# Retention attention: states that change row halves inside their own step, without copies

## The chip, the cores and the metric

One core of one Trainium2 chip runs the whole program. The metric is device microseconds from launch to end; a kernel's time is the median of its runs. The profile is of one execution, whose own time stands beside its span below.

## The reference

Three stages, in fp32:

```
# q, k, v: (4 batches, 8 heads, 576 tokens, 64 dims)
gamma = 1 - 2**(-5 - head)
D     = gamma**(i - j) where i >= j, else 0
attn  = (q @ k.T / 8 * D) @ v                  # retention: causal scores with a decay
x     = attn as (2304 tokens, 512)
h     = x @ w_in                               # 512 -> 2048
x     = (h * clip(h + 3, 0, 6) / 6) @ w_out    # hard-swish MLP, 2048 -> 512
h     = x @ w_in2                              # 512 -> 1024
out   = layer_norm(h * softmax(h)) * g_ln @ w_out2
```

## The kernel before

The 32 heads of all batches are worked on as 16 pairs. A pair's two heads lie in the two row halves (partitions 0 to 63 and 64 to 127; `HEADS` in the code) of the q and k tiles, which hold them transposed. The 576 tokens are cut into chunks of 128 (the last has 64; `CHUNKS`). Inside a chunk the scores are computed and masked; what earlier chunks contribute comes through a 64x64 state per head and chunk: state 0 is u 0, and state c is the state before it, times a decay, plus u c, where u c is the product of chunk c's decayed v and k. The state before a chunk, times the chunk's q, gives the rest of its output.

For each pair `attention()` issues: `scores` (16 matmuls s; ScalarE copies them to st; GpSimd masks st), `load_pair` for the pair three ahead (four DMAs on SyncE's queue: rk, rq, rv, rn), `chunk_states` (matmuls u; VectorE builds state), `prep` (ScalarE scales the next pair's v), `values` of the pair before (matmuls xp<-st), `last_scores` (matmuls z; VectorE writes st4), and `from_states` of the pair before (matmuls xp<-state). VectorE then multiplies xp into xa (L525), ScalarE and GpSimd split xa into two fp32r words, xb (L260, L261), which the first MLP reads. xp, u and z have one PSUM buffer each, so xp of a pair can begin only when xa of the pair before has been taken out, and u when the state chain before has read it.

The output of chunks 1 and 2 is accumulated from the rows of its own head; for chunks 3 and 4 the weights and q lie in the other row half. For chunk 4 the host swaps the halves of q and k. For chunk 3, and for states 2 and 3, VectorE makes the swap with copies into a tile `turned` (lines 461 and 474): two copies of q's chunk 3, and two copies of the two states, a half each.

From pair 2 on, between the pairs, the first MLP's weights are made ready: they come as 64-bit words (wraw, one load for every other pair), ScalarE and VectorE turn them into fp32 (L139, L144, then L147 and L148 on VectorE), and into two fp32r words (L153 on ScalarE, L158 on VectorE or, every third time, on GpSimd). From pair 4 on, six matmuls h of the first MLP are issued with each pair. TensorE's matmuls and most of ScalarE's instructions in this stage keep program order; VectorE's are placed by a scheduler. Pairs 0 to 2 (`early`) are loaded ahead of everything into tiles of another pool. After the attention come the first MLP in token blocks and the second MLP.

Of the kernel before, what the change touches and what calls it, by code (L numbers as in the profile page):

```python
# [9 lines left out]
F32 = mybir.dt.float32  # L10
# [5 lines left out]
ALU = mybir.AluOpType  # L16
AX = mybir.AxisListType

B, H, S, D = 4, 8, 576, 64
NT, DM, DFF, DFF2 = 2304, 512, 2048, 1024  # L20
NH = B * H
NP = DM // 128
# [1 line left out]
NFF2 = DFF2 // 128  # L24
FA = 6
GAMMA = [1.0 - 2.0 ** (-5 - h) for h in range(H)]
N_DEC = H + H // 2 + H // 2
NPAIR = NH // 2
NV = 5
BLOCKS = [(0, 512), (512, 512), (1024, 512), (1536, 512), (2048, 256)]  # L30
# [44 lines left out]
def retention_hardswish_solu_kernel(ctx, tc, kt, qt, kn, vt, w1, w2i, w2o, gln, decay, place, out):  # L75


    nc = tc.nc
    ve, se, ge, te, sy = nc.vector, nc.scalar, nc.gpsimd, nc.tensor, nc.sync
# [301 lines left out]
    pa = tc.alloc_tile_pool(name="pa", bufs=1)  # L381
    ps_a = tc.alloc_tile_pool(name="ps_a", bufs=1, space=bass.MemoryType.PSUM)

    decay_sb = pa.tile([128, N_DEC], F32, name="decay_sb")
    place_sb = p0.tile([128, NP, 128], F32, tag="r", bufs=2, name="place_sb")
# [1 line left out]
    tab_sb = [pa.tile([128, S], F32, name=f"tab_sb{p}") for p in range(NP)]  # L387
    mask4 = pa.tile([128, NP, 64], F32, name="mask4")
    raws, vs, sts, sts4, states, us, xps = {}, {}, {}, {}, {}, {}, {}
    HEADS = [slice(0, 64), slice(64, 128)]  # L390
    CHUNKS = [slice(128 * c, min(128 * c + 128, S)) for c in range(NV)]

    def at_x(c):

        return slice(128 + CHUNKS[c].start, 128 + CHUNKS[c].stop)
# [3 lines left out]
    def mm_a(*args, **kw):  # L399
        keep(nc.tensor.matmul(*args, **kw))  # L400

    def load_pair(pr):

        if pr >= NPAIR:
            return
        early = pr < EARLY
        if early:
            tag = "wi" if pr < 2 else "g"
            rk, rq, rn = [p0.tile([128, n], F32, tag=tag, bufs=FA, name=f"raw{pr}_{i}")
                          for i, n in enumerate((S, S, 512))]  # L410
        else:
            rk = pa.tile([128, S], F32, tag="rk", bufs=3, name=f"rk{pr}")
            rq = pa.tile([128, S], F32, tag="rq", bufs=4, name=f"rq{pr}")
            rn = pa.tile([128, 512], F32, tag="rn", bufs=3, name=f"rn{pr}")
        nc.sync.dma_start(out=rk, in_=kt[pr])
        nc.sync.dma_start(out=rq, in_=qt[pr])
        if early:
            rv = p0.tile([128, 9, D], F32, tag="g", bufs=FA, name=f"rv{pr}")
        else:
            rv = pa.tile([128, 9, D], F32, tag="rv", bufs=3, name=f"rv{pr}")  # L420
        nc.sync.dma_start(out=rv, in_=vt[pr])
        nc.sync.dma_start(out=rn, in_=kn[pr])
        raws[pr] = rk, rq, rn.rearrange("p (c d) -> p c d", d=128), rv

    def prep(pr):
# [13 lines left out]
    def scores(pr):  # L439
# [4 lines left out]
        for c in range(4):  # L444
            for h in range(2):
                mm_a(sp[h][:, CHUNKS[c]], k[HEADS[h], CHUNKS[c]], q[HEADS[h], CHUNKS[c]], start=(c == 0), stop=(c == 3))
        for h in range(2):
# [6 lines left out]
    def chunk_states(pr):  # L454

        rn, v = raws[pr][2], vs[pr]
        up = ps_a.tile([128, 4, 64], F32, tag="u", bufs=1, name=f"u{pr}")
        state = pa.tile([128, 4, 64], F32, tag="state", bufs=2, name=f"state{pr}")
        turned = pa.tile([128, 256], F32, tag="turned", bufs=2, name=f"turned{pr}")
        for h in range(2):  # L460
            ve.tensor_copy(out=turned[HEADS[1 - h], :128], in_=raws[pr][1][HEADS[h], CHUNKS[3]])
        states[pr] = state, turned
        for c in range(4):
            for h in range(2):
                mm_a(up[HEADS[h], c], rn[:, c, HEADS[h]], v[:, 4 * h + c], start=(c == 0), stop=(c == 3))
        at = H + pr % NP
        ve.tensor_copy(out=state[:, 0], in_=up[:, 0])
        for c in range(1, 4):
            ve.scalar_tensor_tensor(  # L469
                out=state[:, c], in0=state[:, c - 1], scalar=decay_sb[:, at:at + 1], in1=up[:, c],  # L470
                op0=ALU.mult, op1=ALU.add,
            )
        for h in range(2):
            ve.tensor_copy(  # L474
                out=turned[HEADS[1 - h], 128:].rearrange("p (c e) -> p c e", e=64), in_=state[HEADS[h], 2:],
            )

    def places():

# [12 lines left out]
    def last_scores(pr):  # L492
# [3 lines left out]
        for h in range(2):  # L496
            mm_a(zp[HEADS[h]], k[HEADS[h], CHUNKS[4]], q[HEADS[h], CHUNKS[4]], start=True, stop=True)
        ve.tensor_tensor(out=st4, in0=zp, in1=mask4[:, pr % NP], op=ALU.mult)

    def values(pr):  # L500
# [3 lines left out]
        for c in range(4):  # L504
            for h in range(2):
                mm_a(xp[HEADS[h], at_x(c)], v[:, 4 * h + c], st[h][:, CHUNKS[c]], start=(c in (0, 3)), stop=False)

    def from_states(pr):
        xp = xps.pop(pr)
        rq, v, (state, turned), st4 = raws.pop(pr)[1], vs.pop(pr), states.pop(pr), sts4.pop(pr)  # L510
        for h in range(2):
            mm_a(xp[HEADS[h], at_x(4)], v[HEADS[1 - h], 8], st4[HEADS[1 - h]], start=False, stop=False)
        for c, w, q in (
            (1, state[:, 0], rq[:, CHUNKS[1]]), (3, turned[:, 128:192], turned[:, :128]),
            (2, state[:, 1], rq[:, CHUNKS[2]]), (4, turned[:, 192:], rq[:, CHUNKS[4]]),
        ):
            for h in range(2):
                r = HEADS[h if c < 3 else 1 - h]
                mm_a(xp[HEADS[h], at_x(c)], w[r], q[r], start=False, stop=(c in (2, 4)))
        evac_x(pr, xp)  # L520

    def evac_x(pr, xp):
        b, p = divmod(pr, NP)
        xa = pa.tile([128, S], F32, tag="xa", bufs=2, name=f"xa{pr}")
        ve.tensor_tensor(out=xa, in0=xp[:, 128:704], in1=tab_sb[p], op=ALU.mult)  # L525
        for t, tc0, s0, m in segments(b * S, S):
            if (t, p) not in xb:
                xb[t, p] = x_tile(t, p)
            split_x(xb[t, p], slice(tc0, tc0 + m), xa[:, s0:s0 + m])

    def attention():

        for pr in range(NPAIR + 1):
            if pr < NPAIR:
                scores(pr)
                idle_mm(N_IDLE.get(pr, 0))
                if pr == 0:
                    places()
                yield pr
                load_pair(pr + EARLY)  # L540
                chunk_states(pr)
                prep(pr + 1)
                if pr < NP:
                    widen(pr)
            if pr:
                values(pr - 1)
            yield pr
            if pr < NPAIR:
                last_scores(pr)
            if pr:  # L550
                from_states(pr - 1)
            yield pr
            if pr == 1:
                tc.keep_in_program_order(nc.sync.dma_start(out=gln_sb, in_=gln))
# [16 lines left out]
    for pr in range(EARLY):  # L571
        load_pair(pr)
# [3 lines left out]
    for h in range(2):  # L576
        ge.affine_select(
            out=mask4[HEADS[h]], in_=mask4[HEADS[h]], compare_op=ALU.is_ge, fill=0.0,
# [115 lines left out]
    last = len(pairs) - 1  # L694
    x2r, x2w, h2, ebuf, stats, us, lnT, turned, lTs = {}, {}, {}, {}, {}, {}, {}, {}, {}
# [215 lines left out]
    ve, se, ge, te, sy = (Pinned(tc, e) for e in (ve, se, ge, te, sy))  # L911
# [59 lines left out]
    for i in range(last + 1):  # L971
        e = [ends[i, p] for p in range(7)]
# [83 lines left out]
```

## Time and profile before

| | |
|---|---|
| runs | 658.96 us median of 3 (658.83 to 660.0) |
| the profiled execution | 659.14 us; its span 657.4 us |
| granted TensorE clock | 1.00 |
| busy in the span | PE 648.0 us (99%), DVE 356.2 (54%), ACT 370.1 (56%), POOL 328.3 (50%) |
| DMA | 112.93 MB, mean 172 GB/s |
| chain that ended last, by engine | PE 89%, DVE 8%, ACT 1%, issue 1% |

PE is TensorE's matmuls, PEld its weight loads, DVE VectorE, ACT ScalarE, POOL GpSimd, SP SyncE. The shares are means over stages; the attention fills about the first 93 us. A busy PE is not PE at its peak, since ends of matmuls are modelled.

### The profile page before, as it was taken

How to read it: one execution, taken by the hardware profiler on the slowest of the kernel's cores; microseconds unless marked ns; L12 is line 12 of the kernel's file. 1: busy time of each engine (PE TensorE's matmuls, PEld its weight loads, DVE VectorE, ACT ScalarE, POOL GpSimd, SP SyncE). 2: the span in 40 equal slices, each digit the busy share in tenths (PEclk: the TensorE clock that was granted, in tenths of full speed). 3: DMA queues.
4: the chain of work that ended last, by engine and by line, in shares of the span. 5: the costliest groups of instructions: out<-in, count | busy, mean ns of one | idle time of the engine just before them, and what ended most of it. 6: DMA issues, size and time to landing. Idle time of an engine off the chain costs nothing.

```text
span 657.4 us, 10671 instructions
## 1 busy us (share of the span) xinstructions
PE 648.0 (99%) x3922; PEld 536.8 (82%) x3922; DVE 356.2 (54%) x666; ACT 370.1 (56%) x653; POOL 328.3 (50%) x342
## 2 busy tenths in 40 slices
PE   9989999999999999999999999999999999999998
PEld 5767778888889988888888888889988888888887
DVE  4888875407111646135465436212487878887750
ACT  5778666538233756146256337305378677778582
POOL 4767662315031425135135004606469899999453
PEclk9999999999999999999999999999999999999999
DMA  9999615449105252367775654239876343534342
GB/s 322 384 277 328 201 63 183 156 134 360 66 0 161 98 161 96 129 220 230 267 251 185 206 178 160 97 121 345 302 194 158 85 105 100 129 81 96 74 100 69
DMA packets 80025, 112.93 MB, mean 172 GB/s; under 512 B 42594, under 2 KB 47458, under 8 KB 79972
## 3 DMA queue, kind: packets, MB, share of 16 engines
q1 hardware_dynamic: 79824, 112.22, 54.1%
q8 instruction: 31, 0.51, 0.3%
q14 instruction: 22, 0.18, 0.1%
q10 hardware_dynamic: 148, 0.01, 0.0%
HBM read 70.80 MB, written 31.98 MB: 156 GB/s over the span
## 4 chain that ended last, share of the span: by engine, by line
PE 89%; DVE 8%; ACT 1%; issue 1%; POOL 0%; DVEq 0%; POOLq 0%; ACTq 0%
PE h L272 28%; PE x L297 20%; PE o L71 15%; PE h L71 13%; PE acc L297 8%; PE x L71 2%; DVE state L469 2%; DVE turned L474 2%; DVE xa L525 1%; DVE wz L148 1%; PE xp L400 1%; PE warm L400 1%; PE s L400 1%; ACT xb L260 1%; DVE w L158 1%
## 5 line engine op out<-in xcount | busy, mean ns | idle before, releaser
L291 POOL TENSOR_TENSOR g<-gf,g 128x512 fp32r<-128x512 f32 (+1 forms) x78 | 96.7, 1240 | 215.6 <-ACT g L290 208.0
L297 PE MATMUL x<-g,w 128*128 128x512 f32 x576 | 132.0, 389 | 0.0
L272 PE MATMUL h<-xb,w 128*128 128x512 f32 (+1 forms) x600 | 130.2, 360 | 1.8 <-POOL w L158 1.8
L297 PEld LDWEIGHTS x<-g,w 128*128 128x128 f32 x576 | 108.1, 188 | 22.5
L272 PEld LDWEIGHTS h<-xb,w 128*128 128x128 f32 x600 | 98.2, 189 | 19.9 <-POOL w L158 2.6
L285 DVE SCALAR_TENSOR_TENSOR gf<-r,h 128x512 f32<-128x512 f32 (+1 forms) x80 | 50.4, 631 | 118.2 <-ACT r L284 104.6
L71 PE MATMUL o<-w,lt 128*128 128x512 f32 (+1 forms) x456 | 103.0, 378 | 0.0
L71 PEld LDWEIGHTS o<-w,lt 128*128 128x128 f32 x456 | 82.4, 188 | 16.3 <-POOL lt L71 0.3
L284 ACT ACTIVATE r<-h,half 128x512 f32<-128x512 f32 (+1 forms) x80 | 50.6, 635 | 63.0 <-PE h L272 63.0
L272 PE MATMUL h<-xB,w 128*128 128x512 f32 x360 | 82.4, 389 | 0.0
L272 PEld LDWEIGHTS h<-xB,w 128*128 128x128 f32 x360 | 67.6, 188 | 14.0
L290 ACT ACTIVATE g<-gf 128x512 fp32r<-128x512 f32 (+1 forms) x78 | 46.1, 591 | 43.4 <-DVE gf L285 38.2
L71 POOL TENSOR_TENSOR lt<-lT,lt 128x512 fp32r<-128x512 f32 x36 | 61.0, 1710 | 13.5 <-ACT lt L71 13.5
L297 PE MATMUL acc<-g,w 128*128 128x512 f32 (+1 forms) x264 | 62.0, 360 | 0.0
L71 ACT ACTIVATE e<-h,stat 128x1024 f32<-128x1024 f32 x36 | 41.3, 1148 | 35.5 <-DVE stat L71 35.3
L297 PEld LDWEIGHTS acc<-g,w 128*128 128x128 f32 x264 | 46.9, 188 | 8.7
L71 PE MATMUL h<-w2t,xt 128*128 128x512 f32 x216 | 53.5, 390 | 0.0
L147 DVE TENSOR_SCALAR wz<-wz 128x512 int32<-128x512 int32 x44 | 28.2, 641 | 40.9 <-ACT wz L139 40.6
L71 PEld LDWEIGHTS h<-w2t,xt 128*128 128x128 f32 x216 | 40.3, 188 | 8.2
L261 POOL TENSOR_TENSOR xb<-xa,xb 128x512 fp32r<-128x512 f32 (+7 forms) x32 | 30.6, 978 | 21.8 <-ACT xb L260 21.8
L71 PE MATMUL h<-w2b,xt 128*128 128x512 f32 x162 | 39.9, 390 | 0.1
L148 DVE CUSTOM_DVE_ANT_0 wz<-wz,wt 128x1024 uint16<-128x1024 uint16 x44 | 36.7, 836 | 5.0
(123 smaller groups left out, 879.7 us busy)
## 6 DMA issues: line engine op xcount, KB each, us to landing
wraw<-in_w_dram SPq DMA_DIRECT2D x32, 512.0 KB, 5.0
xs<-xb SPq DMA_DIRECT2D x12, 512.0 KB, 6.3
xB<-xs SPq DMA_DIRECT2D x12, 512.0 KB, 6.9
rv<-in_vt_dram SPq DMA_DIRECT2D x16, 288.0 KB, 5.3
x2l<-x2s SPq DMA_DIRECT2D x18, 256.0 KB, 3.9
x2f<-x2o SPq DMA_DIRECT2D x18, 256.0 KB, 3.5
x2r<-x2f SPq DMA_DIRECT2D x9, 512.0 KB, 4.0
out_dram<-osb SPq DMA_DIRECT2D x17, 256.0 KB, 2.0
```

The source lines that it names most:

```text
L71: return lambda *args, **kw: self.keep(op(*args, **kw))
L147: ve.tensor_scalar(out=z, in0=z, scalar1=3, scalar2=None, op0=ALU.logical_shift_left)
L148: ve.tensor_tensor(out=z, in0=z, in1=t, op=ALU.add)
L261: ge.tensor_tensor(out=x[:, 1, c], in0=src, in1=f32(x[:, 0, c]), op=ALU.subtract)
L272: mm = nc.tensor.matmul(hp, w1t[ff, 0][:, a, c], xb[t, p][:, b, :n], start=(p == 0 and i == 0), stop=(p == NP - 1 and i == 2),)
L284: se.activation(out=r, in_=hp, func=ACTF.Relu, scale=1.0 / 6.0, bias=half)
L285: ve.scalar_tensor_tensor(out=gf, in0=r, scalar=1.0, in1=hp, op0=ALU.min, op1=ALU.mult)
L290: se.activation(out=g[ff][:, 0], in_=gf, func=ACTF.Copy)
L291: ge.tensor_tensor(out=g[ff][:, 1], in0=gf, in1=f32(g[ff][:, 0]), op=ALU.subtract)
L297: te.matmul(acc, w1t[ff, 1][:, a, c], g[:, b], start=(first and i == 0), stop=(last and i == 2))
L400: keep(nc.tensor.matmul(*args, **kw))
L469: ve.scalar_tensor_tensor(out=state[:, c], in0=state[:, c - 1], scalar=decay_sb[:, at:at + 1], in1=up[:, c], op0=ALU.mult, op1=ALU.add,)
```

## The change

Three things. The u of chunk 3 of a head is put, by the matmul's output columns, into the other row half of the PSUM tile. The step from state 1 to state 2 is done in two half instructions, each reading one row half (state 1, u 2 and the decay) and writing state 2 into the other; the step to state 3 then runs in full width in the swapped halves, with a decay table that the host has swapped too (four more columns of `decay`). And q's chunk 3 with swapped halves is a further 128 columns of q in DRAM: a pair's q is 704 columns wide instead of 576. For pairs 3 to 15 these come with the same DMA; for pairs 0 to 2 they are a DMA of their own behind the pair's other four. The tile `turned` and its copies are gone.

```diff
-            rq = pa.tile([128, S], F32, tag="rq", bufs=4, name=f"rq{pr}")
+            rq = pa.tile([128, S + 128], F32, tag="rq", bufs=4, name=f"rq{pr}")
...
-        nc.sync.dma_start(out=rq, in_=qt[pr])
+        n = S if early else S + 128
+        nc.sync.dma_start(out=rq[:, :n], in_=qt[pr][:, :n])
...
         nc.sync.dma_start(out=rn, in_=kn[pr])
+        if early:
+            nc.sync.dma_start(out=rq[:, n:], in_=qt[pr][:, n:])
...
-        turned = pa.tile([128, 256], F32, tag="turned", bufs=2, name=f"turned{pr}")
-        for h in range(2):
-            ve.tensor_copy(out=turned[HEADS[1 - h], :128], in_=raws[pr][1][HEADS[h], CHUNKS[3]])
...
-                mm_a(up[HEADS[h], c], rn[:, c, HEADS[h]], v[:, 4 * h + c], start=(c == 0), stop=(c == 3))
+                o = HEADS[1 - h if c == 3 else h]
+                mm_a(up[o, c], rn[:, c, HEADS[h]], v[:, 4 * h + c], start=(c == 0), stop=(c == 3))
...
-        for c in range(1, 4):
-            ve.scalar_tensor_tensor(
-                out=state[:, c], in0=state[:, c - 1], scalar=decay_sb[:, at:at + 1], in1=up[:, c],
-                op0=ALU.mult, op1=ALU.add,
-            )
-        for h in range(2):
-            ve.tensor_copy(
-                out=turned[HEADS[1 - h], 128:].rearrange("p (c e) -> p c e", e=64), in_=state[HEADS[h], 2:],
-            )
+        for c, to, at in (
+            (1, ((ALL, ALL),), H + pr % NP), (2, tuple(zip(HEADS, HEADS[::-1])), H + pr % NP),
+            (3, ((ALL, ALL),), H + 2 * NP + pr % NP),
+        ):
+            for i, o in to:
+                ve.scalar_tensor_tensor(
+                    out=state[o, c], in0=state[i, c - 1], scalar=decay_sb[i, at:at + 1], in1=up[i, c],
+                    op0=ALU.mult, op1=ALU.add,
+                )
...
-            (1, state[:, 0], rq[:, CHUNKS[1]]), (3, turned[:, 128:192], turned[:, :128]),
-            (2, state[:, 1], rq[:, CHUNKS[2]]), (4, turned[:, 192:], rq[:, CHUNKS[4]]),
+            (1, state[:, 0], rq[:, CHUNKS[1]]), (3, state[:, 2], rq[:, S:]),
+            (2, state[:, 1], rq[:, CHUNKS[2]]), (4, state[:, 3], rq[:, CHUNKS[4]]),
...
+    qt = np.concatenate([qt, np.roll(qt[:, :, 384:512], D, axis=1)], axis=2)
```

Apart from these instructions the order on each engine is the same in both kernels. On VectorE, around the state chain of pair 6 (numbers behind names are tile numbers), before:

```order
L461 COPY turned_705<-rq_424 64x128 x2
L158 TENSOR_TENSOR w_1_0_663<-wz,w_1_0_663 128x512
L285 SCALAR_TENSOR_TENSOR gf_0_673<-r_0_672,h_0_578 128x512
L467 COPY state_704<-u_703 128x64
L469 SCALAR_TENSOR_TENSOR state_704<-state_704,decay_sb,u_703 128x64 x3
L498 TENSOR_TENSOR st_744<-z_743,mask_116 128x64
L474 COPY turned_705<-state_704 64x128 x2
L525 TENSOR_TENSOR xa_758<-xp_726,tab_sb_113 128x576
```

and after:

```order
L158 TENSOR_TENSOR w_1_0_642<-wz,w_1_0_642 128x512
L285 SCALAR_TENSOR_TENSOR gf_0_652<-r_0_651,h_0_561 128x512
L466 COPY state_683<-u_682 128x64
L472 SCALAR_TENSOR_TENSOR state_683<-state_683,decay_sb,u_682 128x64
L472 SCALAR_TENSOR_TENSOR state_683<-state_683,decay_sb,u_682 64x64 x2
L472 SCALAR_TENSOR_TENSOR state_683<-state_683,decay_sb,u_682 128x64
L497 TENSOR_TENSOR st_719<-z_718,mask_116 128x64
L524 TENSOR_TENSOR xa_733<-xp_701,tab_sb_113 128x576
```

Four copies a pair are gone, and one step has become two half steps; nothing else has changed places. On SyncE's queue, at the program's start, before:

```order
L415 DMA raw_0_134<-in_kt_dram 128x576
L416 DMA raw_1_135<-in_qt_dram 128x576
L421 DMA rv_139<-in_vt_dram 128x576
L422 DMA raw_2_136<-in_kn_dram 128x512
L415 DMA raw_0_142<-in_kt_dram 128x576
```

and after:

```order
L415 DMA raw_0_134<-in_kt_dram 128x576
L417 DMA raw_1_135<-in_qt_dram 128x576
L422 DMA rv_139<-in_vt_dram 128x576
L423 DMA raw_2_136<-in_kn_dram 128x512
L425 DMA raw_1_135<-in_qt_dram 128x128
L415 DMA raw_0_143<-in_kt_dram 128x576
```

Three such DMAs, one behind each of the first three pairs, stand ahead of all later loads.

## Rows read from the trace of the kernel before

**Rows 1.** Stretches: start:end, length, busy us (count) PE PEld DVE ACT POOL, clock, DMA share, GB/s.
```profile
10.00:20.00 10.00, 10.00 (x202) 8.17 (x203) 8.03 (x28) 7.45 (x17) 6.06 (x13) 1.00 1.05 396
...
50.00:60.00 10.00, 9.99 (x156) 7.86 (x156) 8.59 (x22) 6.87 (x17) 6.33 (x8) 1.00 0.94 337
...
92.00:140.00 48.00, 48.00 (x238) 39.21 (x234) 20.67 (x30) 25.78 (x46) 16.07 (x13) 1.00 0.39 131
```

**Rows 2.** Chain that ended last, 48 to 64 us, by line.
```profile
by line: DVE turned L474 20.4%; DVE wz L148 17.1%; DVE state L469 16.2%; DVE xa L525 14.4%; issue 7.8%; ACT xb L260 6.5%; DVE w L158 5.3%; PE xp L400 3.8%; DVE gf L285 3.7%; ACT w L153 3.3%; DVE turned L461 2.8%; DVE wz L147 2.7%; DVE state
```

**Rows 3.** VectorE in order of time: start, us, engine, line, what [idle before <-releaser].
```profile
55.75 0.76 DVE L525 TENSOR_TENSOR xa<-xp,tab_sb 128x576 f32<-128x576 f32 x1
56.54 0.46 DVE L461 COPY turned<-rq 64x128 f32<-64x128 f32 x2
57.87 0.84 DVE L158 TENSOR_TENSOR w<-wz,w 128x512 fp32r<-128x512 f32 x1 [0.88 <-ACT w L153]
...
59.23 0.21 DVE L467 COPY state<-u 128x64 f32<-128x64 f32 x1
59.48 0.91 DVE L469 SCALAR_TENSOR_TENSOR state<-state,decay_sb,u 128x64 f32<-128x64 f32 x3
...
60.54 1.44 DVE L474 COPY turned<-state 64x128 f32<-64x128 f32 x2
62.01 0.76 DVE L525 TENSOR_TENSOR xa<-xp,tab_sb 128x576 f32<-128x576 f32 x1
...
63.85 1.31 DVE L148 CUSTOM_DVE_ANT_0 wz<-wz,wt 128x1024 uint16<-128x1024 uint16 x1
```

**Rows 4.** TensorE in order of time, same columns.
```profile
30.52 1.66 PE L272 MATMUL h<-xb,w 128*128 128x512 f32 x6
...
35.50 1.75 PE L272 MATMUL h<-xb,w 128*128 128x512 f32 x6
...
53.28 1.66 PE L272 MATMUL h<-xb,w 128*128 128x512 f32 x6
...
60.51 1.64 PE L400 MATMUL s<-rq,rk 64*128 64x128 f32 x16 [0.48 <-ACT st L448]
...
64.64 1.66 PE L272 MATMUL h<-xb,w 128*128 128x512 f32 x6
...
87.27 4.41 PE L272 MATMUL h<-xb,w 128*128 128x512 f32 x18
```

**Rows 5.** ScalarE in order of time, same columns.
```profile
59.34 0.63 ACT L290 ACTIVATE g<-gf 128x512 fp32r<-128x512 f32 x1 [0.93 <-DVE gf L285]
59.88 1.06 ACT L448 ACTIVATE st<-s 128x512 f32<-128x512 f32 x2
...
62.44 0.67 ACT L144 ACTIVATE wt<-wraw 128x512 int32<-128x512 uint32 x1
```

**Rows 6.** Instructions on the tile turned: duration ns min/median/max, first and last start.
```profile
L474 DVE COPY turned<-state x32: 220/341/949, 10.8 to 89.5; 64x128 f32<-64x128 f32 x32
L461 DVE COPY turned<-rq x26: 219/222/328, 18.7 to 85.7; 64x128 f32<-64x128 f32 x26
```

**Rows 7.** Instructions on the tile state, same columns.
```profile
L469 DVE SCALAR_TENSOR_TENSOR state<-state,decay_sb,u x48: 272/281/285, 9.9 to 88.4; 128x64 f32<-128x64 f32 x48
```

**Rows 8.** GpSimd in order of time, columns as rows 3.
```profile
60.05 1.27 POOL L291 TENSOR_TENSOR g<-gf,g 128x512 fp32r<-128x512 f32 x1 [0.88 <-ACT g L290]
...
63.61 2.02 POOL L261 TENSOR_TENSOR xb<-xa,xb 128x384 fp32r<-128x384 f32 x2 [1.12 <-ACT xb L260]
```

**Rows 9.** All engines in order of time, 18 to 21 us, columns as rows 3.
```profile
18.31 0.70 ACT L139 ACTIVATE wz<-wraw 128x512 f32<-128x512 f32 x1 [0.28 <-DMA wraw<-in_w_dram]
...
19.91 0.69 DVE L148 CUSTOM_DVE_ANT_0 wz<-wz,wt 128x1024 uint16<-128x1024 uint16 x1
...
20.20 1.81 POOL L261 TENSOR_TENSOR xb<-xa,xb 128x512 fp32r<-128x512 f32 x2 [1.22 <-ACT xb L260]
```

**Rows 10.** Who waited for whom, 12 to 86 us: in total, times, longest.
```profile
ACT wz L139 <- DMA wraw<-in_w_dram: 0.3, 1, 0.3
```

More of the change, by code (lines that the diff above doesn't have):

```diff
@@ L26 @@
 GAMMA = [1.0 - 2.0 ** (-5 - h) for h in range(H)]
-N_DEC = H + H // 2 + H // 2
+N_DEC = H + H // 2 + H // 2 + H // 2
 NPAIR = NH // 2
@@ L389, in retention_hardswish_solu_kernel @@
     raws, vs, sts, sts4, states, us, xps = {}, {}, {}, {}, {}, {}, {}
-    HEADS = [slice(0, 64), slice(64, 128)]
+    HEADS, ALL = [slice(0, 64), slice(64, 128)], slice(0, 128)
     CHUNKS = [slice(128 * c, min(128 * c + 128, S)) for c in range(NV)]
@@ L409, in load_pair @@
             rk, rq, rn = [p0.tile([128, n], F32, tag=tag, bufs=FA, name=f"raw{pr}_{i}")
-                          for i, n in enumerate((S, S, 512))]
+                          for i, n in enumerate((S, S + 128, 512))]
         else:
             rk = pa.tile([128, S], F32, tag="rk", bufs=3, name=f"rk{pr}")
-            rq = pa.tile([128, S], F32, tag="rq", bufs=4, name=f"rq{pr}")
+            rq = pa.tile([128, S + 128], F32, tag="rq", bufs=4, name=f"rq{pr}")
             rn = pa.tile([128, 512], F32, tag="rn", bufs=3, name=f"rn{pr}")
         nc.sync.dma_start(out=rk, in_=kt[pr])
-        nc.sync.dma_start(out=rq, in_=qt[pr])
+        n = S if early else S + 128
+        nc.sync.dma_start(out=rq[:, :n], in_=qt[pr][:, :n])
         if early:
@@ L457, in chunk_states @@
         up = ps_a.tile([128, 4, 64], F32, tag="u", bufs=1, name=f"u{pr}")
-        state = pa.tile([128, 4, 64], F32, tag="state", bufs=2, name=f"state{pr}")
-        turned = pa.tile([128, 256], F32, tag="turned", bufs=2, name=f"turned{pr}")
-        for h in range(2):
-            ve.tensor_copy(out=turned[HEADS[1 - h], :128], in_=raws[pr][1][HEADS[h], CHUNKS[3]])
-        states[pr] = state, turned
+        state = states[pr] = pa.tile([128, 4, 64], F32, tag="state", bufs=2, name=f"state{pr}")
         for c in range(4):
             for h in range(2):
-                mm_a(up[HEADS[h], c], rn[:, c, HEADS[h]], v[:, 4 * h + c], start=(c == 0), stop=(c == 3))
-        at = H + pr % NP
+                o = HEADS[1 - h if c == 3 else h]
+                mm_a(up[o, c], rn[:, c, HEADS[h]], v[:, 4 * h + c], start=(c == 0), stop=(c == 3))
         ve.tensor_copy(out=state[:, 0], in_=up[:, 0])
-        for c in range(1, 4):
-            ve.scalar_tensor_tensor(
-                out=state[:, c], in0=state[:, c - 1], scalar=decay_sb[:, at:at + 1], in1=up[:, c],
-                op0=ALU.mult, op1=ALU.add,
-            )
-        for h in range(2):
-            ve.tensor_copy(
-                out=turned[HEADS[1 - h], 128:].rearrange("p (c e) -> p c e", e=64), in_=state[HEADS[h], 2:],
-            )
+        for c, to, at in (
[7 more added lines that the diff above has]
+                )
     def places():
@@ L509, in from_states @@
         xp = xps.pop(pr)
-        rq, v, (state, turned), st4 = raws.pop(pr)[1], vs.pop(pr), states.pop(pr), sts4.pop(pr)
+        rq, v, state, st4 = raws.pop(pr)[1], vs.pop(pr), states.pop(pr), sts4.pop(pr)
         for h in range(2):
@@ L1041 @@
     last = np.concatenate([last[:64, :, 1], last[64:, :, 0]], axis=0)
-    place, decay = place.astype(np.float32), np.concatenate([over, step, last], axis=1).astype(np.float32)
+    place, decay = place.astype(np.float32), np.concatenate([over, step, last, np.roll(step, D, axis=0)], axis=1).astype(np.float32)
     host = dict(kt=kt, qt=qt, kn=kn, vt=vt, w1=w1, w2i=w2i, w2o=w2o, gln=gln, decay=decay, place=place)
```

## The prediction

> **What bounds the kernel now.** I read the stretches first, to see where TensorE has anything to give. Behind the attention, from 92 to 140 us, PE is busy for 48.00 of 48.00 us [rows 1], and the view of waits names none of PE's behind that: no saving on another engine helps there, but whatever the attention gives up moves the whole rest forward. In the attention PE looks busy too, 9.99 of 10 us from 50 to 60 [rows 1], but a busy PE need not be at its pace; the pace shows in when the same work comes round. Six matmuls h stand once in each pair. From 30.52 to 35.50 a pair takes 4.98 us; the two pairs from 53.28 to 64.64 take 11.36 us together, not 9.96 [rows 4]. From 30.52 to 87.27 there are eleven such groups, so ten pairs in 56.75 us; at 4.98 each they would take 49.8. So 6.95 us can be had there at most, and nothing after.
>
> Next I read the chain, to see what the lost time waits for. From 48 to 64 us it runs mostly on VectorE: turned L474 20.4%, wz L148 17.1%, state 16.2%, xa 14.4% [rows 2]. So, although VectorE is busy for only 8.59 of 10 us [rows 1], its order is the loop that sets the pace. The place where TensorE feels it is in every second pair: s waits 0.48 us for ScalarE's st, and its 16 matmuls then take 1.64 us [rows 4], since the second half of st comes later still. Followed back: st (59.88) stands behind g, which waited 0.93 us for VectorE's gf [rows 5]; gf stands behind w L158, which waited for ScalarE's w, which comes after xa of the pair before [rows 3]. So xa's end sets the time of the next st, and the copies ahead of xa set xa.
>
> **The change, part by part.**
>
> *The copies go.* The two of q's chunk 3 take 0.46 us a pair, the two of the states 1.44 us in the slow pair [rows 3]; the state copies have a median of 341 ns each, a least of 220 and a most of 949 [rows 6]. The long one starts at 60.54, while GpSimd works from 60.05 to 61.32 [rows 8], and the pair of copies ends at 61.98. The steps of the state, which read PSUM besides, took 272 to 285 ns in all 48 cases [rows 7], whatever GpSimd did. So the copies' price is partly a wait for GpSimd, which the half steps should not have.
>
> [...]
>
> *The half steps come.* One step of about 0.31 us with its gap (three take 0.91) becomes two, with half the rows but the same 64 elements along each. I take 0.31 for each; a half step below the least row, 0.22 of a copy across the halves [rows 6], or above 0.86, which a copy needs against GpSimd, would surprise me. So the chain grows from 1.16 us (59.23 to 60.39) to 1.47 [rows 3].
>
> [...]
>
> *Per pair on VectorE:* less 0.46 and 0.57 to 1.44, plus 0.31: 0.7 to 1.6 us off.
>
> *What is late next.* For two pairs, let xa's end (55.75 + 0.76 = 56.51) be zero. ScalarE's chain behind it (xb, w, r, g, st, v, wz, wt) does not get shorter: w and gf hang on xa, not on the copies, and wt ends at 62.44 + 0.67 = 63.11 [rows 3, 5], 6.60 us later. Then L148 can start; before, it started at 63.85, since the copies held VectorE. Behind it come the state chain, 1.47, and with their gaps the mask of z and xa, about 1.0. With L148 at 0.69 the loop is 6.60 + 0.05 + 0.69 + 1.47 + 1.0 = 9.8 us; with L148 at 1.31 it is 10.4. L148 took 0.69 at 19.91, where GpSimd began its xb after it, at 20.20 [rows 9], and 1.31 at 63.85, where GpSimd had begun at 63.61 [rows 3, 8]. After the change L148 is about 0.7 us earlier, and xb on GpSimd is not, since it follows wt on ScalarE; so the row at 19.91 is nearer. TensorE itself needs 9.96 for two pairs. The slower of the two loops decides: 9.96, or 10.4 where GpSimd still wins. I take 10.1. Five times (11.36 - 10.1) is 6.3 us; the ends are 5 x 0.96 = 4.8 and the whole 6.95.
>
> *The u of chunk 3 in the other columns* is as many matmuls as before. The head that comes first now takes the columns that the matmul just ahead of it used. The trace shows no such neighbours. If it must wait for a whole matmul, I estimate the price from s, 16 rows in 1.64 us [rows 4], 0.10 each and twice as wide as u: at most 0.05 a pair, 0.8 us over 16 pairs; at least nothing. I take 0.2.
>
> *The q from DRAM.* 64 KB more for each pair, 1 MB in all. At the start the queue is full: share 1.05, 396 GB/s [rows 1]. Ahead of the first wraw stand three extra DMAs and one longer one, 256 KB or 0.66 us at that rate; as the early ones move rows of only 512 bytes I allow 0.8. ScalarE already waits 0.28 us for that wraw at 18.31 [rows 9], so its wz, and st and s behind it, come up to 0.8 later. TensorE loses that at pair 4; but soon after it needs the first w from VectorE, which hangs on the xa before it, now free of its copies. So most of the 0.8 is hidden there; I charge 0.3, with 0 and 0.8 as ends. Later loads have cover: this was the one wait for a load from 12 to 86 us [rows 10], and a pair is loaded three pairs ahead, some 15 us. SyncE issues three DMAs more, ahead of the other loads, with the queue full anyway. The four more decay columns are 2 KB: nothing.
>
> *Sum:* 6.3 - 0.2 - 0.3 = 5.8 us. The profiled execution took 659.14, its span 657.4; it becomes 653.3. The median, 658.96, is 0.2 lower, so I predict 653.2, a span near 651.6.
>
> **The rivals.**
>
> *GpSimd keeps the lock (22%).* L148 still meets xb in most turns, so the loop is 10.4, and neither the wraw nor the columns are hidden: 4.8 - 0.8 - 0.8 = 3.2 us, 655.9. For it: at 63.85 L148 took 1.31, and a shift of a tenth decides which of two engines is first. Against: wt, not the copies, should now release L148, and xb follows wt.
>
> *All is hidden (10%).* TensorE runs at 4.98 from the start, and pairs 3 to 5, ahead of 30.52, give up 1 us more (at the 0.7 a pair of the later ones they would give 2): 8 us, 651.2. Against: the late wraw.
>
> *The loads become the bound (6%), the other side.* The DMA share is 0.94 at 337 GB/s from 50 to 60 us [rows 1]. If the queue is really full through the attention, each pair's 64 KB costs 0.19 us at that rate, 16 pairs 3.1 us, and the pairs can be no closer than the loads let them: 659.1 + 3.1 = 662.2. It decides from the point where a pair's q lands after its first s. Against: only 0.3 us of waits for loads in all [rows 10].
>
> *Off the path (7%).* The attention ends earlier, but the weights of the second half (wraw, ScalarE, VectorE) do not follow, and TensorE waits for them instead: 659. Against: from 92 to 140 us VectorE is busy for 20.67 of 48 us and DMA at 0.39 [rows 1], and they shift with the attention.
>
> **How the numbers follow.** My own case has 55%, from 651.9 to 654.9 (a gain of 4 to 7). The 80% range reaches into both neighbours: 651.0 to 657.0. About 0.2%, 1.3 us, is what a measurement here can tell from no change. Faster: 0.55 + 0.22 + 0.10, 0.87; the same, mostly the fourth rival, 0.07; slower 0.06.
>
> **What would show it.** In the new profile: no gaps of 0.48 before s in every second pair, and groups of h about 10.1 us apart over two pairs; L148 at about 0.7, started right behind wt; half steps near 0.28; the first wz at about 19.0 instead of 18.31; a PE still without gaps from 87 us on. The prediction is wrong if h stays at 11 us for two pairs (then ScalarE's chain, not VectorE's, was the loop), if s waits for rq or rk, or if gaps open on PE behind 92 us.

## The result, and the profile after

The changed kernel takes 651.04 us (median of 4 runs, 650.53 to 651.58); the kernel before took 658.89 us on the same chip (median of 4 runs; the table above has the first 3). The ratio is 0.9877 [0.9860, 0.9894]: a gain of 7.8 us, where 5.8 were forecast, and the median lies at the lower edge of the range (651.0), 0.9 us below the own case of the forecast (651.9 to 654.9). In a later comparison on another chip the ratio was 0.9875 [0.9862, 0.9887]. The profiled execution took 651.58 us, its span 649.8.

Stretches of the changed kernel, in the columns of [rows 1]:

```profile
50.00:60.00 10.00, 10.00 (x169) 7.86 (x157) 7.08 (x20) 8.68 (x20) 7.41 (x11) 1.00 0.99 337
...
92.00:140.00 48.00, 47.99 (x210) 39.02 (x209) 17.82 (x27) 26.05 (x45) 11.90 (x9) 1.00 0.49 165
```

PE's busy time says as little as before; VectorE is busy for 7.08 us instead of 8.59, and the rest behind the attention is still full. The groups of h show what happened (TensorE in order of time, against [rows 4]):

```profile
30.66 1.66 PE L272 MATMUL h<-xb,w 128*128 128x512 f32 x6
35.54 1.66 PE L272 MATMUL h<-xb,w 128*128 128x512 f32 x6
...
79.40 4.47 PE L272 MATMUL h<-xb,w 128*128 128x512 f32 x18
```

From there every pair takes 4.87 us, none more. The ten pairs from 30.66 to 79.40 take 48.74 us; before they took 56.75. That is 8.0 us; 0.14 was lost ahead of the first of them, and 0.3 behind the last, so the span is 7.6 shorter.

The chain that ended last, 48 to 64 us, by line, in place of [rows 2]:

```profile
by line: PE h L272 29.8%; PE xp L400 29.6%; PE s L400 21.2%; PE u L400 15.4%; PE z L400 4.7%
```

VectorE is gone from it: TensorE waits for nobody. VectorE's own order over one turn of two pairs, against [rows 3]:

```profile
50.38 0.76 DVE L524 TENSOR_TENSOR xa<-xp,tab_sb 128x576 f32<-128x576 f32 x1
52.50 0.83 DVE L158 TENSOR_TENSOR w<-wz,w 128x512 fp32r<-128x512 f32 x1 [1.36 <-ACT w L153]
...
57.20 0.43 DVE L147 TENSOR_SCALAR wz<-wz 128x512 int32<-128x512 int32 x1 [1.09 <-ACT wz L139]
57.77 0.69 DVE L148 CUSTOM_DVE_ANT_0 wz<-wz,wt 128x1024 uint16<-128x1024 uint16 x1 [0.15 <-ACT wt L144]
58.45 0.23 DVE L466 COPY state<-u 128x64 f32<-128x64 f32 x1
58.71 1.21 DVE L472 SCALAR_TENSOR_TENSOR state<-state,decay_sb,u 128x64 f32<-128x64 f32 x4
...
60.12 0.76 DVE L524 TENSOR_TENSOR xa<-xp,tab_sb 128x576 f32<-128x576 f32 x1
```

L148 took 0.69 here, before 1.31, and it waits for ScalarE's wt, as does L147 for wz: in this turn the idle 1.09 us are VectorE's reserve. All seven of L148 from 12 to 86 us (groups of instructions by line: count, busy us, mean ns, idle before):

```profile
L148 DVE CUSTOM_DVE_ANT_0 wz<-wz,wt 128x1024 uint16<-128x1024 uint16 x7 | 4.8, 693 | 1.0 <-ACT wt L144 0.3
```

What ScalarE and then GpSimd do there (in order of time, in the columns of [rows 5] and [rows 8]):

```profile
57.06 0.68 ACT L144 ACTIVATE wt<-wraw 128x512 int32<-128x512 uint32 x1
```

```profile
58.24 1.66 POOL L261 TENSOR_TENSOR xb<-xa,xb 128x384 fp32r<-128x384 f32 x2 [1.10 <-ACT xb L260]
```

L148 began at 57.77, ahead of GpSimd's xb at 58.24; before, 0.24 behind it. The steps of the state, against [rows 7]:

```profile
L472 DVE SCALAR_TENSOR_TENSOR state<-state,decay_sb,u x64: 272/281/289, 9.8 to 79.1; 128x64 f32<-128x64 f32 x32, 64x64 f32<-64x64 f32 x32
```

The half steps (64x64) cost what the full ones cost: four follow one another in 1.21 us, 0.30 each. And the one place where the change lost (all engines in order of time, 18 to 22 us, against [rows 9]):

```profile
19.27 0.68 ACT L139 ACTIVATE wz<-wraw 128x512 f32<-128x512 f32 x1 [0.76 <-DMA wraw<-in_w_dram]
...
21.73 0.48 PE L400 MATMUL s<-rq,rk 64*128 64x128 f32 x2 [1.15 <-ACT st L451]
```

The first wraw is there at 19.27 instead of 18.31, and the st and s behind it on their engines are late with it.

### The profile page after: what moved, and what is told of

Its sections match the earlier page's. It is cut to its first block, busy times and chain, and to the rows that moved or that the text cites. A ratio compares the mean times of both kernels' runs of the same rounds, so it can differ in the third digit from the quotient of the medians.

```text
span 649.8 us, 10629 instructions
## 1 busy us (share of the span) xinstructions
PE 643.9 (99%) x3922; PEld 535.0 (82%) x3922; DVE 334.3 (51%) x618; ACT 370.9 (57%) x653; POOL 325.2 (50%) x342
## 4 chain that ended last, share of the span: by engine, by line
PE 96%; DMA 3%; ACT 0%; SPq 0%; issue 0%; ACTq 0%
PE h L272 31%; PE x L297 20%; PE o L71 15%; PE h L71 13%; PE acc L297 8%; PE xp L400 3%; PE x L71 2%; PE s L400 2%; DMA wraw<-in_w_dram 1%; PE u L400 1%; DMA raw<-in_qt_dram 1%; DMA raw<-in_kn_dram 1%; PE z L400 0%; ACT wt L144 0%; ACT xb L260 0%
## 5 line engine op out<-in xcount | busy, mean ns | idle before, releaser
L147 DVE TENSOR_SCALAR wz<-wz 128x512 int32<-128x512 int32 x44 | 28.8, 653 | 47.0 <-ACT wz L139 46.7
L139 ACT ACTIVATE wz<-wraw 128x512 f32<-128x512 f32 x44 | 29.1, 662 | 18.1 <-DMA wraw<-in_w_dram 9.2
L261 POOL TENSOR_TENSOR xb<-xa,xb 128x512 fp32r<-128x512 f32 (+7 forms) x32 | 28.2, 902 | 16.3 <-ACT xb L260 16.3
```

Source lines behind the costliest of these rows:

```text
L139: first = se.activation(out=z.bitcast(F32), in_=raw[:, :, 1].bitcast(F32), func=ACTF.Prelu, scale=2.0 ** -112, alpha=2.0 ** 32)
L147: ve.tensor_scalar(out=z, in0=z, scalar1=3, scalar2=None, op0=ALU.logical_shift_left)
L261: ge.tensor_tensor(out=x[:, 1, c], in0=src, in1=f32(x[:, 0, c]), op=ALU.subtract)
```

## The experiments

Theory: the gain is VectorE's time on the loop xa, ScalarE, L148, states, xa, part of it time in which the copies wait for GpSimd; the floor under it is TensorE's own pace. Against it stand: the wait for GpSimd is all of it; it is VectorE's time alone, wherever it stands; TensorE gained from what it reads (it no longer reads `turned`); the loads are the floor. Letters in the expectations are those of each text. Times of before are of the same chip as the run beside them.

**One part alone, q.** The q of chunk 3 comes from DRAM; the copies of the states stay (the diff is against the kernel before):

```diff
-            ve.tensor_copy(out=turned[HEADS[1 - h], :128], in_=raws[pr][1][HEADS[h], CHUNKS[3]])
...
-            (1, state[:, 0], rq[:, CHUNKS[1]]), (3, turned[:, 128:192], turned[:, :128]),
+            (1, state[:, 0], rq[:, CHUNKS[1]]), (3, turned[:, :64], rq[:, S:]),
```

> Only the q part of the change: q's chunk 3 from DRAM, the two copies of the states stay. Theory (VectorE's own time ahead of xa sets the pace of two pairs): L148 no longer comes after the q copies, so two pairs take about 10.3 us instead of 11.36, and the time is 653.5 (653 to 654.5). Rival A (the wait for GpSimd in the state copies is nearly all of the gain): these copies still wait, two pairs stay above 11 us, 657 to 659. Rival B (TensorE gains because it no longer reads the tile turned): about half of the gain, 655.

653.89 us against 659.07, ratio 0.9924 [0.9909, 0.9939]. As the theory had it. VectorE around the turn of L148 (in order of time):

```profile
59.85 0.69 DVE L148 CUSTOM_DVE_ANT_0 wz<-wz,wt 128x1024 uint16<-128x1024 uint16 x1
...
60.72 0.92 DVE L470 SCALAR_TENSOR_TENSOR state<-state,decay_sb,u 128x64 f32<-128x64 f32 x3
...
61.78 0.86 DVE L475 COPY turned<-state 64x128 f32<-64x128 f32 x2
62.67 0.76 DVE L526 TENSOR_TENSOR xa<-xp,tab_sb 128x576 f32<-128x576 f32 x1
```

Without the copies of q, L148 has its 0.69 already: from 12 to 86 us it is never longer in this kernel.

**The other part alone, states and columns.** The half steps and the u columns; the two copies of q stay (the diff is against the changed kernel):

```diff
+            ve.tensor_copy(out=turned[HEADS[1 - h]], in_=raws[pr][1][HEADS[h], CHUNKS[3]])
...
-            (1, state[:, 0], rq[:, CHUNKS[1]]), (3, state[:, 2], rq[:, S:]),
+            (1, state[:, 0], rq[:, CHUNKS[1]]), (3, state[:, 2], turned),
```

> Only the state part: half steps and the u of chunk 3 in the other columns; q's two copies on VectorE stay, and no byte more is loaded. Theory: the loop is the changed kernel's 9.75 plus the 0.46 us of the q copies, about 10.2 for two pairs, 653; nothing is lost to loads at the start, so the first h stands no later than the 25.34 of before. Rival A: the wait for GpSimd is gone with the state copies, so nearly the whole gain, 651.3. Rival B: about half, 655.

657.52 us, 0.9973 [0.9962, 0.9983]: above all the numbers given; the h of pair 4 stands at 25.48, not by 25.34. VectorE in order of time shows why:

```profile
51.33 0.69 DVE L148 CUSTOM_DVE_ANT_0 wz<-wz,wt 128x1024 uint16<-128x1024 uint16 x1
...
52.19 1.20 DVE L474 SCALAR_TENSOR_TENSOR state<-state,decay_sb,u 128x64 f32<-128x64 f32 x4
...
53.54 1.15 DVE L461 COPY turned<-rq 64x128 f32<-64x128 f32 x2
54.72 0.76 DVE L526 TENSOR_TENSOR xa<-xp,tab_sb 128x576 f32<-128x576 f32 x1
```

The scheduler put q's copies directly ahead of xa. There the two take 1.15 us, where before, behind xa, they took 0.46 [rows 3]. So this run is no clean removal of one part: it removed the state copies and moved q's to their place. The gains of the parts, 5.2 and 1.6 us, don't add up to 7.8 for that reason.

**Copies put back that nobody reads**, two a pair ahead of xa, once from SBUF and once from PSUM:

```diff
+        for h in range(2):
+            ve.tensor_copy(out=turned[HEADS[1 - h], :].rearrange("p (c e) -> p c e", e=64), in_=state[HEADS[h], 2:])
```

> The changed kernel, plus two copies a pair of states 2 and 3 from the state tile into a tile that nobody reads, at the place where the state copies stood. Theory: VectorE has 1.8 us of idle time to spare in two pairs, but the copies stand ahead of xa: two pairs take 10.2 to 10.6, 653 to 655. Rival A: the copies wait for GpSimd again, up to 0.95 us each, and the time is 656 or more. Rival B: nobody reads the copies on TensorE, so 651.0 as the changed kernel.

```diff
+        for h in range(2):
+            ve.tensor_copy(out=turned[HEADS[1 - h], :].rearrange("p (c e) -> p c e", e=64), in_=up[HEADS[h], 2:])
```

> As the one before, but the two copies read u 2 and u 3 in PSUM, not the state tile in SBUF. Theory: a copy from PSUM should not wait for GpSimd and takes about 0.25 us in every case; what it adds is VectorE's own time, 0.5 a pair, so the time is at or slightly below the kernel with SBUF copies, 652 to 654. Rival A: without the wait for GpSimd no loss at all, 651.0. Rival B: 651.0 too.

From SBUF 657.79 us, 0.9984 [0.9975, 0.9994], above the theory's range: here rival A's number came, 656 or more. From PSUM 654.16, 0.9924 [0.9909, 0.9939], 0.2 above the theory's range and far from the 651.0 of both rivals. The copies (duration ns min/median/max), of the first kernel and of the second:

```profile
L478 DVE COPY turned<-state x32: 220/570/679, 10.0 to 86.9; 64x128 f32<-64x128 f32 x32
```

```profile
L478 DVE COPY turned<-u x32: 283/288/294, 11.3 to 83.3; 64x128 f32<-64x128 f32 x32
```

VectorE and GpSimd of the SBUF version, then of the PSUM version, in the same turn (st's mask stands ahead of the copies in the first, behind them in the second):

```profile
60.05 1.15 DVE L478 COPY turned<-state 64x128 f32<-64x128 f32 x2
```

```profile
59.27 1.27 POOL L291 TENSOR_TENSOR g<-gf,g 128x512 fp32r<-128x512 f32 x1 [0.89 <-ACT g L290]
60.50 1.22 POOL L452 TENSOR_SCALAR_AFFINE_SELECT st<-st 128x512 f32<-128x512 f32 x2
```

```profile
58.13 0.59 DVE L478 COPY turned<-u 64x128 f32<-64x128 f32 x2
```

```profile
57.49 1.29 POOL L291 TENSOR_TENSOR g<-gf,g 128x512 fp32r<-128x512 f32 x1 [0.89 <-ACT g L290]
58.73 1.22 POOL L452 TENSOR_SCALAR_AFFINE_SELECT st<-st 128x512 f32<-128x512 f32 x2
```

In both GpSimd works on through the copies. From SBUF they take 1.15 us, from PSUM 0.59, although a copy from SBUF alone is the shorter one (220 ns against 283). So it is through most of the attention: from 30 to 80 us the 18 copies from SBUF took 574 ns in the mean, the 20 from PSUM 289. Where no GpSimd instruction ran beside them, two copies from SBUF took 0.46 us in the kernel before (56.54 to 57.00 [rows 3]; GpSimd in order of time):

```profile
54.19 1.22 POOL L449 TENSOR_SCALAR_AFFINE_SELECT st<-st 128x512 f32<-128x512 f32 x2
57.15 2.03 POOL L261 TENSOR_TENSOR xb<-xa,xb 128x384 fp32r<-128x384 f32 x2 [1.74 <-ACT xb L260]
```

The two kernels differ by 3.6 us in all: nearly all of it is the price of waiting for GpSimd, more than the theory gave it. The other 3.1 us, from 651.04 to 654.16, are VectorE's time itself, so the wait is not all. Nothing reads these copies: what they cost does not come from TensorE's reading. Why a copy from SBUF takes longer beside GpSimd, no run shows; the wait for GpSimd is a name for that longer time. The pair of runs shows where it comes: same work, same turn, and copies from SBUF take 220 to 679 ns each, while those from PSUM are never stretched (283 to 294 ns).

**All four copies back, unread.**

```diff
+            ve.tensor_copy(out=turned[HEADS[1 - h]], in_=raws[pr][1][HEADS[h], CHUNKS[3]])
...
+            ve.tensor_copy(out=turned[HEADS[1 - h], :].rearrange("p (c e) -> p c e", e=64), in_=state[HEADS[h], 2:])
```

> The changed kernel, with all four copies a pair put back as work that nothing reads: two of q's chunk 3 and two of states 2 and 3, SBUF to SBUF on VectorE, at the places of before. Theory (the gain is VectorE's time and its wait for GpSimd, and nothing else of the change matters): the whole gain goes, two pairs take about 11.3 us again, 658.2 to 660. Rival (what TensorE reads, the u columns, or the loads gave part of it): some of the gain stays, 656.5 or less.

667.77 us against 658.82, 1.0138 [1.0121, 1.0155]: slower than before by 9 us, with the same four copies. Neither number came. The copies did not come back to their places (VectorE in order of time):

```profile
61.93 0.46 DVE L463 COPY turned<-rq 64x128 f32<-64x128 f32 x2
62.42 0.76 DVE L529 TENSOR_TENSOR xa<-xp,tab_sb 128x576 f32<-128x576 f32 x1
64.54 0.82 DVE L158 TENSOR_TENSOR w<-wz,w 128x512 fp32r<-128x512 f32 x1 [1.36 <-ACT w L153]
```

The q copies now stand ahead of xa. Before, they stood behind it, in front of a w that VectorE had to wait 0.88 us for anyway [rows 3], so that one pair in two had them for nothing; now the idle time of 1.36 behind xa stays empty. Two pairs take 12.2 us (a table further below adds up to it). So it is not VectorE's time wherever it stands: nearly the same work in another order is worth 9 us. Half of these are at the start, where h of pair 4 comes at 29.90 us instead of 25.34 (TensorE waited 1.65 and then 1.92 us for xa there; behind the second wait xp took 1.35 us and that h 2.36, one pair later 1.05 and 1.66; the mean granted clock of that execution was 0.997); VectorE waited for loads of q ahead of an xa that needed none (in order of time):

```profile
20.21 0.80 DVE L463 COPY turned<-rq 64x128 f32<-64x128 f32 x2 [1.17 <-DMA rq<-in_qt_dram]
21.04 0.76 DVE L529 TENSOR_TENSOR xa<-xp,tab_sb 128x576 f32<-128x576 f32 x1
```

**More bytes.** Pairs 3 to 15 load 48 KB more each, which nothing reads:

```diff
-            rq = pa.tile([128, S + 128], F32, tag="rq", bufs=4, name=f"rq{pr}")
+            rq = pa.tile([128, S + 224], F32, tag="rq", bufs=4, name=f"rq{pr}")
...
-        n = S if early else S + 128
+        n = S if early else S + 224
```

> The changed kernel itself, unaltered, on the same chip as the next three, as their yardstick. 651.0 us, within 0.5.

> The changed kernel, but the q of pairs 3 to 15 is loaded 96 columns wider still, 48 KB a pair that nothing reads: 0.62 MB more. Theory (4.87 us a pair is TensorE's own pace, and the loads have room below it): h stays 4.87 apart, 651.0, at most 0.3 more at the start. Rival (the loads already set the pace): at the 337 to 359 GB/s of the attention 48 KB take 0.14 us, 13 pairs 1.8 us: 652.8, with waits of s for rq.

The changed kernel again: 650.95 us. With 48 KB more: 650.83, both 0.9875 of before (659.17). Stretch 30 to 70 us, of the changed kernel's first profile and of the wider one:

```profile
30.00:70.00 40.00, 40.00 (x652) 31.86 (x651) 27.65 (x76) 34.45 (x79) 31.16 (x40) 1.00 1.02 364
```

```profile
30.00:70.00 40.00, 40.00 (x631) 31.92 (x630) 27.64 (x74) 34.73 (x80) 31.19 (x41) 1.00 1.02 380
```

A DMA share of 1.02 looks full, and yet 4% more bytes went through and cost nothing: the loads are not the floor. In the four kernels with copies, too, of one or the other kind, the quicker pair of two takes 4.87 us; only in the two kernels with all four copies it takes more.

**The start.** Five kernels that try to win back what the late first wraw costs, by two remedies and both together.

> The changed kernel, but pairs 0 to 2 get their swapped q by two VectorE copies each, as before the change, instead of the three 64 KB DMAs; so 192 KB less stand ahead of the first wraw. Theory (the bytes at the start cost what the attention's start lost): wraw lands about 0.5 us earlier, near 18.7 instead of 19.2; TensorE's wait for st, 1.15 us near 20.6, shrinks by 0.3 to 0.6; every h from pair 4 on comes that much earlier and the pace of 4.87 stays: 650.4 to 650.8. Rival A (that wait comes from elsewhere, the v that waits for rv): time as the changed kernel's, 651.0. Rival B (six copies on VectorE cost more than the bytes): 651.3 or more.

> As the run before, and the first conversion of wraw on ScalarE (wz, wt) is issued behind the next pair's st copy, no longer ahead of it, so that st and TensorE's scores do not stand behind the wait for wraw. Theory (the wait of 1.15 us near 20.6 us is a queue on ScalarE, not a need of data): the wait goes, and every later h comes 0.8 to 1.2 us earlier than in the changed kernel: 649.8 to 650.3. Rival (the first w is then late, and the first h waits for it instead): a new PE wait for w near 24 us, and 651 or more.

> The changed kernel, but the first conversion of wraw (wz, wt on ScalarE) is issued behind the st of pair 3, no longer ahead of it. Theory (TensorE's wait for st near 20.5 us, 0.64 to 1.15 in three profiles of this design, is a queue on ScalarE behind a late load): the wait goes, and with the pace unchanged all that follows comes 0.5 to 1.0 us earlier: 650.0 to 650.4. Rival (the first w, which the first h needs, is then late): a PE wait for w near 25 us of about the same size, 650.8 or more.

> The changed kernel, but pairs 0 to 2 get the swapped q by two ScalarE copies each, issued behind their st copies, where q has long landed, instead of the three 64 KB DMAs. It is the version with VectorE copies with its own fault taken out: there the third copy stood at the head of VectorE's queue waiting for its load, and TensorE waited 3.48 us. Theory (192 KB less ahead of the first wraw): wraw lands 0.5 us earlier, the wait for st at 20.5 us shrinks by about that: 650.4 to 650.7. Rival (six ScalarE copies of about 0.3 us each delay v and st by more than that): 651 to 652.

> Both of the last two: ScalarE copies for pairs 0 to 2 and the first wz behind the st of pair 3. Theory: no wait of TensorE between 5 and 480 us beyond 0.2 us, 649.8 to 650.4; if the first is right and the second wrong, as the late wz alone.

The edits: the first inserts VectorE copies and drops the early DMA, the fourth the same on ScalarE; the third moves the first `wq.begin()`; the second and fifth combine.

```diff
-        if early:
-            nc.sync.dma_start(out=rq[:, n:], in_=qt[pr][:, n:])
...
+                ve.tensor_copy(out=q[HEADS[1 - h], S:], in_=q[HEADS[h], CHUNKS[3]])
```

```diff
-        if pr >= W_FROM and pr % 2 == 0 and s % 3 == 1:
+        if (pr > W_FROM and pr % 2 == 0 and s % 3 == 1) or (pr == W_FROM + 1 and s % 3 == 0):
```

```diff
+                keep(se.activation(out=q[HEADS[1 - h], S:], in_=q[HEADS[h], CHUNKS[3]], func=ACTF.Copy))
```

With VectorE copies 654.48 us (0.9928 [0.9915, 0.9941]), and with the late wz besides 655.14 (0.9943 [0.9931, 0.9955]): 3.5 and 4.2 us slower than the changed kernel: the numbers of the rivals that lie above, but the cause is neither's. VectorE and then TensorE of the first of these:

```profile
11.24 0.81 DVE L462 COPY raw<-raw 64x128 f32<-64x128 f32 x2 [1.98 <-DMA raw<-in_qt_dram]
11.97 0.21 DVE L468 COPY state<-u 128x64 f32<-128x64 f32 x1
```

```profile
13.81 0.79 PE L400 MATMUL u<-v,raw 128*64 128x64 f32 x16 [3.48 <-DVE state L474]
14.32 1.98 PE L400 MATMUL xp<-st,v 128*64 128x128 f32 x16
```

The scheduler let the copy for pair 2 stand at the head of VectorE's queue, where it waits for a load that lands at 11.2, ahead of a state chain whose u was long there; TensorE stood still for 3.48 us. Behind that its granted clock was lower (third column from the end, 15 to 20 us):

```profile
15.00:20.00 5.00, 5.00 (x85) 4.20 (x81) 2.55 (x9) 2.64 (x7) 0.78 (x1) 0.73 1.04 397
```

The xp at 14.32 took 1.98 us; in the changed kernel, with a granted clock of 1.00 from 10 to 20 us, it took 1.04.

With the late wz alone 650.51 us (0.9875 [0.9861, 0.9890]), with ScalarE copies 650.42 (0.9872 [0.9858, 0.9887]), with both 650.78 (0.9877 [0.9863, 0.9892]). The second lies in its theory's range, the first just above it, the third misses it: TensorE waited there 0.28 us for v and 0.60 for xa instead. Two medians lie 0.4 to 0.5 below the changed kernel's 650.95, but no ratio can be told from its 0.9875. In the late-wz kernel s no longer waits for st, 1.15 us in the first profile of the changed kernel (TensorE in order of time):

```profile
20.44 1.16 PE L400 MATMUL s<-rq,rk 64*128 64x128 f32 x16 [0.44 <-DMA rq<-in_qt_dram]
```

It waits for its load instead, 0.44 us. So the queue on ScalarE held st, and the loads stand right behind it. Whether the start can give 0.5 us stays open: in three profiles of the changed start (its two and the wider one's) the h of pair 4 came at 25.62, 25.18 and 24.97 us, which is as much as what was looked for.

## Why the prediction was right in kind and short in size

*The loop was right, and after the change it no longer binds.* From xa's end (51.14) to wt's end (57.74) are 6.60 us, as forecast; with L148 0.69, the state chain 1.47 (58.45 to 59.92) and mask and xa, the next xa ends at 60.88: 9.74 us for two pairs, where 9.8 was worked out for an L148 of 0.69. That these 9.74 are also TensorE's 9.75 is no accident: VectorE waits for TensorE in this turn. The xa at 60.12 stands 0.15 us behind the end of the last xp (TensorE in order of time):

```profile
59.37 0.60 PE L400 MATMUL xp<-rq,state 64*64 64x128 f32 x16
```

So do, by 0.15 to 0.16, all four xa behind an L148 from 50 to 80 us. How long the loop is by itself can be estimated from the kernel with PSUM copies, where xa comes 1.3 us or more after xp and L148 starts right behind wt: 10.18 less its 0.59 of copies is 9.59. To this estimate the other kernels add what they put into the turn of L148 (the one of two pairs in which it stands), and the time by which L148 starts later behind wt than in the changed kernel, since copies in the other turn, or q's copies ahead of L147, use up more than the wait for wz (1.09 us here):

| kernel | us more in the L148 turn | L148 later | 9.59 + both | measured, two pairs |
|---|---|---|---|---|
| changed | 0 | 0 | 9.59 | 9.75 (TensorE's pace) |
| states' copies, 3 steps | 0.86 - 0.30 | 0.14 | 10.29 | 10.31 |
| PSUM copies | 0.59 | 0 | 10.18 (taken from it) | 10.18 |
| SBUF copies | 1.15 | 0.12 | 10.86 | 10.91 |
| q's copies ahead of xa | 1.15 | 0.12 | 10.86 | 10.92 |
| all four copies back | 1.65 | 0.95 | 12.19 | 12.21 |
| before | 0.65 - 0.30, L148 0.69 longer | 0.73 | 11.36 | 11.38 |

(Means of four turns of L148 from 38 to 84 us; measured: eight pairs of h from 30.3 to 35.5 us on, a quarter of them.) All but the changed kernel agree to 0.06, and kernels in which TensorE reads `turned` follow the same sum as those in which nobody does. The last row is the change itself: of what it took from VectorE's loop, 0.73 us is the later start of L148, 0.69 its stretch beside GpSimd, and 0.35 the state copies less the half step.

*The failed step is "I take 10.1"* for the two pairs, a value between 9.96 and 10.4. The L148 of 1.31, from which the 10.4 came, did not occur in the attention: of all kernels run, L148 was stretched ahead of 86 us only in the two with all four copies, and wt releases it now, as the text itself argued. Measured were 9.75, so this choice is 0.35 too long, five times 1.75 us: 0.21 from the floor of 9.96, and 0.14 put on top for an L148 of 1.31.

*Under it lay a wrong floor.* The 4.98 us of the quicker pair [rows 4] was taken as TensorE's own pace. It is 4.87: also the quicker pair of before held 0.11 us of stall, not listed as a wait. TensorE in order of time, before and then after, at the start and in a quick pair:

```profile
14.90 0.69 PE L400 MATMUL u<-v,raw 128*64 128x64 f32 x16
15.42 1.04 PE L400 MATMUL xp<-st,v 128*64 128x128 f32 x16
...
33.20 0.69 PE L400 MATMUL u<-v,rn 128*64 128x64 f32 x16
33.77 1.09 PE L400 MATMUL xp<-st,v 128*64 128x128 f32 x16
```

```profile
14.59 0.69 PE L400 MATMUL u<-v,raw 128*64 128x64 f32 x16
15.11 1.04 PE L400 MATMUL xp<-st,v 128*64 128x128 f32 x16
...
57.71 0.69 PE L400 MATMUL u<-v,rn 128*64 128x64 f32 x16
58.23 1.05 PE L400 MATMUL xp<-st,v 128*64 128x128 f32 x16
```

From u to xp it is 0.52 us at the start in both, but 0.57 in the quick pair of before and 0.52 in that of after; xp, too, runs 0.04 longer before. That is most of the 0.11. What held xp there is VectorE's xa, which must have emptied xp's only PSUM buffer (VectorE of before):

```profile
32.87 0.76 DVE L525 TENSOR_TENSOR xa<-xp,tab_sb 128x576 f32<-128x576 f32 x1
```

It ends at 33.63, and xp starts 0.14 us later. In before all ten xp from 33.77 to 85.55 start 0.14 or 0.15 us behind the end of an xa, in the quick pairs too; the changed kernel's start 1.87 us or more behind it, from 33.86 on. So the prediction's reading that TensorE feels VectorE "in every second pair" missed that it did so in every pair, and in two of the five slow pairs it was not s but h that waited, 0.92 and 0.83 us, for the w of L158 on GpSimd. The "6.95 us at most" was no ceiling; 8.0 came. After the change the slower of the two loops is TensorE's, 9.75 us for two pairs.

*Charges.* The u columns, 0.2: nothing, u to xp is 0.52 us in both kernels. The bytes at the start, 0.3: from 0.28 later to 0.37 earlier at the h of pair 4, no cost that can be told. The half steps at 0.31: 0.30. The first wz at "about 19.0": 19.27. The 0.14 allowed for short rows: in the changed kernel's trace one of the 384 packets of 512 bytes took 27 ns in the median, one of 2304 bytes 93, so per byte the short ones took 1.3 times as long.

*Sum as it should have been:* 5 x (11.36 - 9.75) is 8.05, less 0.14 at the start and 0.3 behind, 7.6 in the span, 7.8 in the medians.

*Rivals.* That GpSimd holds L148 at 1.31 (22%) did not happen: L148 took 0.69 from 12 to 86 us. The lock in that rival's name was the author's reading; the runs show durations alone. "All is hidden" gave 651.2, the nearest number, but by another way: it let pairs 3 to 5 give up 1 us, which they did not, and kept the 4.98. "Off the path" fell, PE is full behind 92 us. The loads fell by the run with more bytes.

## What to carry to other kernels

The best turn of a trace gives an upper bound on the time that an engine needs for a turn, not that time: look inside the turn for matmuls that start later than their kind does elsewhere, and for instructions that always start the same short time behind one of another engine (here xp 0.14 us behind xa); such a wait need not be listed. Count a VectorE instruction only if it lies in the turn that closes the loop, and count it with the time it takes against GpSimd at that place (here 0.57 us for a copy from SBUF instead of 0.22); what stands ahead of a wait that comes anyway costs nothing until it is moved or fills the wait. Before putting back or taking out one part alone, look where the scheduler puts the rest: two of these runs measured a new order, not the part.

## What the runs showed of the hardware

An fp32 copy of 64x128 from SBUF took 0.22 us where GpSimd was idle (56.54 us in the kernel before), 0.57 where it was at work (60.05 us in the SBUF version) and 0.95 at most (the kernel before); the same copy from PSUM 0.28 to 0.29 in all 32 cases, also with GpSimd at work (58.13 us in the PSUM version). A step that reads one row half and writes the other took 0.27 to 0.29 us, like one that stays, and with half the rows it was no quicker (128x64 and 64x64 in the same 272 to 289 ns). The DMA share, at 1.02, let 380 GB/s through (48 KB more) as well as 364 (the changed kernel): a share of one was not a full queue there.
